# Raw key weights fetched first, three large and 46 small unread products at the start, and a new order for the first 428 operations

## The chip, the core and the metric

The kernel runs on one core of one Trainium2 chip. Five engines work side by side, each on its own list of instructions and in the order of that list: TensorE (PE, matrix products; its weight loads are shown apart as PEld), VectorE (DVE), ScalarE (ACT), GpSimd (POOL) and SyncE (SP, which here issues all transfers). An instruction whose data are not there holds everything behind it on its engine. The metric is the device time of one execution in microseconds; smaller is better.

## What is computed

```python
def phi(x):                                   # features, 64 per position
    a = np.einsum('rd,bhsd->bhsr', S1, x)
    b = np.einsum('rd,bhsd->bhsr', S2, x)
    return np.einsum('bhsi,bhsj->bhsij', a, b).reshape(*x.shape[:-1], r * r)
q_p, k_p = phi(q), phi(k)                     # 4 batches, 4 heads, 1088 positions, 32 wide
kv = np.einsum('bhsf,bhsd->bhfd', k_p, v)
z = np.sum(k_p, axis=2)
x = (q_p @ kv) / (q_p . z + 1e-6)             # heads side by side: 4 x 1088 x 128
h = np.maximum(x @ w_in, 0.0)                 # 128 -> 1024
u, v = h[..., :512], h[..., 512:]
v_n = (v - mean(v)) / np.sqrt(var(v) + 1e-6)  # over the 512
v_s = np.einsum('ts,bsd->btd', w_spatial, v_n) + b_spatial[None, :, None]
out = (u * v_s) @ w_out                       # 512 -> 128
```

`S1`, `S2`, `w_in` and `w_out` arrive as 64-bit floats and are turned into 32-bit ones on the chip; "raw key weights" are `S1` and `S2` in that raw form.

## The kernel before

**Tiling.** Positions are tiles of 128 (nine, the last one half real), three of them to a group g. The outer loop is over the four batches. In batch 0 the chain is: key tiles (`kt0g`) times the weights `sk` (product `kab0g`, L747), a copy (`ka0g`, ACT, L752), features (`kp0g`, DVE, L754), the sum over values (`kv0`, L784), masked into `kd0`; the same for queries (`qab`, `qa`, `qp`), then transposes (`tq`, L833), sums and denominators (`nd`, L847), division (`rec`, `x32`), and x as a high and a low part (`xh0`, `xl0`, L865 and L866). Almost every operand that a product reads is such a pair, made by a cast on ACT and a subtraction on DVE or POOL, and a product is three passes: high-high, high-low, low-high.

The hidden layer gives `pv` (the half that is normalised, one product triple per tile) and `pu` (the other half, one per 128 columns d). `vt` is `pv` after the rectifier (ACT), `st` and `mv` its statistics (DVE, L959, L960), then it is normalised (DVE L995 or ACT L998) and split into `vh` (ACT, L1064) and `vl` (DVE, L1067), one tile of positions at a time for batch 0; the second half of the last tile gets the rest in L1076.

**The spatial product** is the bulk of PE's work: `sp0dc` sums over nine position tiles kt for each column block d (4) and each of three pieces c of the output positions. For batch 0 and c = 0 the four d run side by side in four PSUM banks: first the steps with `vh` and `vl` against the high weights (L1123, L1125), one step of two products per kt and d, the ninth with one product; then those with the low weights (L1132). The transposed spatial weights come in blocks `wt{kt}{c}`, each cast to `wTh` (ACT, L720) and subtracted to `wTl` (DVE or POOL, L724). For c = 1 and 2 and for batches 1 to 3 the d follow each other.

**What sets the order.** Each operation is recorded with its engine, a cost and what it reads and writes. `schedule` then plays the five engines forward and appends, again and again, the operation that can start first; among those that could start nearly together on an engine the due number decides. Due numbers come from two lists of names: `ORDER` for the first 428 operations (up to the first products of batch 0's second piece), free within the slack, and `THEN` for all others, each bound to its engine and its place there. Costs, the transfer rate (`RATE`, `SLOW_AT`, `LATENCY`) and the eight transfers in flight decide what "can start first" means. When PE would wait, the planner puts in filler products that nobody reads (`fill`, L608), as many as it thinks fit. So the program's order on each engine is fixed when it is built; on the chip only waits happen.

**The start.** Two memsets make `z9`; PE multiplies it `N_WARM` times by itself (L596, 128 x 128) and then `N_SMALL` times in 32 x 32 corners (L601); these and the fillers are read by nobody. The raw weights `s_raw` go through seven DVE steps (L643 to L656) to `sk`, which the first projection `kab00` needs with the first key tile. The second half of `w_in` (`wi_raw1`, `wi_x1`) takes the same seven steps on 512 columns; its first half (`wi_raw0`) is loaded into the buffers of the three key tiles once `kab02` has read them, and `w_out` (`wo_raw`, `wo_x`) into them later. The bias row `b32` is split into `bh` and `bl` and sent to the last low weights by two transfers. All 32-bit products that are not split run as two passes on PE, so the trace counts twice as many.

## Time and profile before

| what | before |
|---|---|
| runs, us | 324.51, 324.68, 328.12; median 324.68 |
| the profiled execution, us | 326.01 |
| its span, first to last instruction, us | 324.2 |
| PE busy | 317.2 us, 98% |
| PEld busy | 301.8 us, 93% |
| DVE busy | 226.2 us, 70% |
| ACT busy | 164.8 us, 51% |
| POOL busy | 64.5 us, 20% |
| moved by DMA | 26.82 MB, mean 83 GB/s |

Busy shares are means over the whole span, while the change lies in its first fifth, so stretches of it have to be read one by one. A matmul's end is modelled and matmuls overlap, so a busy PE can still be waiting in part; start-to-start times of the same product, early and late, tell more. An instruction of DVE or ACT overlaps the next by about 0.1 us, so its own time counts from its start to the next one's start ("at pitch").

### The profile page before, as it was taken

What the parts mean: (1) busy time and instruction counts of PE and PEld (TensorE: products, weight loads), DVE (VectorE), ACT (ScalarE), POOL (GpSimd) and SP (SyncE); (2) the same over time, 40 slices, a digit from 0 to 9 for tenths busy, and PEclk for the clock granted to TensorE, in tenths of its full rate; (3) what the DMA queues carried; (4) which work ended last, traced back from release to release, by engine and by line L of the source; (5) the groups of instructions that cost most, each with busy time, mean ns of one, the idle gap of its engine ahead of it and who ended that gap; (6) DMA issues with size and microseconds to landing.
All of it is one profiled execution on the core that took longest, in us unless ns stands there. A gap on an engine that the chain in (4) does not pass through costs nothing.

```text
span 324.2 us, 6830 instructions
## 1 busy us (share of the span) xinstructions
PE 317.2 (98%) x2636; PEld 301.8 (93%) x2636; DVE 226.2 (70%) x512; ACT 164.8 (51%) x391; POOL 64.5 (20%) x81
## 2 busy tenths in 40 slices
PE   8999999999999999999999999999999999999995
PEld 7887999899998999999899999999999999999995
DVE  3999995646799962889884658895325687439382
ACT  3499935525785626566544567462424455416040
POOL 1000005566201035321004702240001321103000
PEclk9999999999999999999999999999999999999999
DMA  7873229462010473011043115001000421000001
GB/s 237 289 243 129 53 58 337 142 209 73 21 52 20 129 230 126 2 40 31 14 120 121 61 51 168 0 2 42 3 0 0 128 64 42 2 1 2 0 1 69
DMA packets 21548, 26.82 MB, mean 83 GB/s; under 512 B 2828, under 2 KB 21260, under 8 KB 21516
## 3 DMA queue, kind: packets, MB, share of 16 engines
q1 hardware_dynamic: 21516, 26.39, 26.1%
q8 instruction: 20, 0.33, 0.4%
q14 instruction: 12, 0.10, 0.1%
HBM read 23.31 MB, written 3.06 MB: 81 GB/s over the span
## 4 chain that ended last, share of the span: by engine, by line
PE 77%; DVE 7%; ACT 6%; DMA 6%; issue 2%; SPq 1%; POOL 0%; POOLq 0%; DVEq 0%; ACTq 0%
PE sp L1123 15%; PE sp L1125 13%; PE sp L1132 13%; PE sd L1357 4%; DMA pl<-in_wT 4%; PE sp L1357 3%; PE sd L573 3%; PE sd L575 3%; PE sd L574 3%; PE pu L573 2%; PE po L574 2%; PE po L573 2%; PE pu L575 2%; PE pu L574 2%; PE po L575 2%; PE sp L1134 2%
## 5 line engine op out<-in xcount | busy, mean ns | idle before, releaser
L1123 PE MATMUL sp<-wTh,vh 128*128 128x332 f32 (+1 forms) x350 | 115.0, 329 | 0.0
L1125 PE MATMUL sp<-wTh,vl 128*128 128x332 f32 (+1 forms) x304 | 99.1, 326 | 0.0
L1123 PEld LDWEIGHTS sp<-wTh,vh 128*128 128x128 f32 x350 | 65.8, 188 | 2.6 <-issue 1.2
L1132 PE MATMUL sp<-wl,vh 128*128 128x332 f32 x192 | 59.9, 312 | 0.0
L1125 PEld LDWEIGHTS sp<-wTh,vl 128*128 128x128 f32 x304 | 57.1, 188 | 0.7
L1132 PE MATMUL sp<-wTl,vh 128*128 128x424 f32 x112 | 37.1, 349 | 0.0
L660 ACT CAST g<-u 128x332 fp32r<-128x332 f32 (+1 forms) x41 | 19.8, 490 | 32.5 <-DVE u L1160 22.3
L1132 PEld LDWEIGHTS sp<-wl,vh 128*128 128x128 f32 x192 | 36.0, 188 | 0.0
L583 DVE TENSOR_TENSOR g<-u,g 128x332 fp32r<-128x332 f32 (+1 forms) x41 | 23.1, 562 | 18.0 <-PE po L574 11.4
L1160 DVE TENSOR_TENSOR u<-sp,u 128x332 f32<-128x332 f32 (+1 forms) x43 | 22.4, 521 | 15.9 <-PE sp L1134 9.5
L933 DVE RECIPROCAL c<-c 128x384 f32<-128x384 f32 (+1 forms) x9 | 21.8, 2419 | 16.3 <-ACT c L931 16.3
L1115 ACT ACTIVATE u<-pu 128x332 f32<-128x332 f32 (+1 forms) x44 | 20.6, 469 | 22.2 <-PE pu L575 17.7
L1036 ACT CAST vh<-vt 128x384 fp32r<-128x384 f32 x36 | 17.3, 511 | 20.7 <-DVE vt L995 11.7
L902 POOL TENSOR_TENSOR pl<-pl,pl 128x384 f32<-128x384 f32 (+1 forms) x18 | 18.1, 1007 | 39.6 <-DMA pl<-qd 39.6
L959 DVE BATCH_NORM_STATS2 st<-vt 128x6 f32<-128x512 f32 x36 | 24.0, 684 | 2.2 <-ACT vt L957 1.9
L586 POOL TENSOR_TENSOR r<-pl,r 128x384 fp32r<-128x384 f32 (+1 forms) x18 | 17.7, 986 | 38.3 <-ACT r L660 36.1
L957 ACT ACTIVATE vt<-sd 128x512 f32<-128x512 f32 x36 | 21.4, 603 | 7.5 <-PE sd L575 6.7
L1038 DVE TENSOR_TENSOR vl<-vt,vh 128x384 fp32r<-128x384 f32 (+1 forms) x36 | 18.1, 512 | 5.3 <-ACT vh L1036 5.2
L1132 PEld LDWEIGHTS sp<-wTl,vh 128*128 128x128 f32 x112 | 21.0, 188 | 0.1
L724 POOL TENSOR_TENSOR wl<-pl,wTh 128x332 fp32r<-128x332 f32 x8 | 7.5, 953 | 49.8 <-ACT wTh L720 49.7
L573 PE MATMUL pu<-xh,wih 128*128 128x332 f32 (+1 forms) x48 | 16.5, 343 | 0.0
L995 DVE TENSOR_SCALAR vt<-vt,mv,sm 128x512 f32<-128x512 f32 x32 | 16.4, 557 | 0.0
(287 smaller groups left out, 668.1 us busy)
## 6 DMA issues: line engine op xcount, KB each, us to landing
pl<-in_wT SPq DMA_DIRECT2D x34, 166.0 KB
v<-in_vA SPq DMA_DIRECT2D x12, 198.0 KB
kt<-in_kT SPq DMA_DIRECT2D x12, 192.0 KB
pl<-qd SPq DMA_DIRECT2D x12, 192.0 KB
pl<-qd SPq DMA_DIRECT2D x24, 96.0 KB
c<-in_qT SPq DMA_DIRECT2D x9, 192.0 KB
wl<-in_wT SPq DMA_DIRECT2D x8, 212.0 KB
out<-u SPq DMA_DIRECT2D x6, 166.0 KB
```

The costliest lines, as they stand in the source:

```text
L573: nc.tensor.matmul(o, ah, bh, start=start, stop=False)
L574: nc.tensor.matmul(o, ah, bl, start=False, stop=False)
L575: nc.tensor.matmul(o, al, bh, start=False, stop=stop)
L583: return lambda: nc.vector.tensor_tensor(out=o(), in0=a(), in1=bb(), op=ALU.subtract)
L933: op("DVE", 135 + 6.3 * n, lambda x32=x32, n=n: nc.vector.reciprocal(out=x32[:, :n], in_=x32[:, :n]), w=[x32])
L957: op("ACT", c_act(512, True), lambda pv=pv, t=t: nc.scalar.activation(vt[:, t], pv.ap, AF.Relu), r=[pv], w=[(vt, t)])
L959: op("DVE", 690, lambda stats=stats, t=t: nc.vector.bn_stats(out=stats.ap, in_=vt[:, t]), r=[(vt, t)], w=[stats])
L1123: nc.tensor.matmul(sp[:, :cw], vh[:, kt], wTh[:, kt, cs], start=(kt == begin), stop=False)
L1125: nc.tensor.matmul(sp[:, :cw], vl[:, kt], wTh[:, kt, cs], start=False, stop=False)
L1132: nc.tensor.matmul(sp[:, :cw], vh[:, kt], w_lo(kt, c), start=False, stop=False)
L1160: op("DVE", c_dve(cw), lambda: nc.vector.tensor_tensor(out=u.ap, in0=sp[:, :cw], in1=u.ap, op=ALU.mult), r=[sp], w=[u], lead=LEAD[1])
L1357: nc.tensor.matmul(x[:, :cw], p, q, start=i == 0 and n == 0, stop=end and i == 3 and n == 2)
```

## The change

Five edits, all in what the planner is given; no operation of the computation is added or taken away.

- `N_WARM` goes from five to three, `N_SMALL` from 36 to 46.
- The planner's model of transfers: a higher rate, one rate for the transfers through DRAM, and a list of pauses in place of one late slow-down.
- The planner's cost of the small products, of the first projection, and the size of `w_in`'s transfers.
- `ORDER`, the 428 names, is another list. `THEN` is the same.

```diff
-N_WARM = 5
-N_SMALL = 36
+N_WARM = 3
+N_SMALL = 46
...
-kt00:1 z9:1 eps:2 z9:2 s_raw:1 eps:1 v93:1 wps:1 v90:1 kt01:1 wps:2 v92:1 v91:1 wps:3 wi_raw1:1 wps:4
+s_raw:1 z9:1 eps:2 z9:2 kt00:1 eps:1 v92:1 wps:1 v91:1 kt01:1 wps:2 v93:1 v90:1 wps:3 b32:1 wps:4
...
-RATE, SLOW_AT, SLOW_BY, LATENCY = 0.265, 4000, 500, 1500
+RATE, BOUNCE, LATENCY = 0.38, 0.13, 1500
+PAUSES = ((3500, 1050), (8000, 900), (13000, 1400), (18000, 1400), (49000, 900), (51800, 800), (57200, 2000))
...
-                dma = max(dma, s + cost + LATENCY) + o.kb / (RATE if o.kb > 0 else -0.12)
+                dma = max(dma, s + cost + LATENCY) + o.kb / (RATE if o.kb > 0 else -BOUNCE)
...
-                if dma > SLOW_AT and not slow:
-                    slow, dma = True, dma + SLOW_BY
+                while pauses and dma > pauses[0][0]:
+                    dma += pauses.pop(0)[1]
...
-    op("PE", 1300, f4=True, fn=small, r=[z9], w=[wps], due=0)
+    op("PE", 1770, f4=True, fn=small, r=[z9], w=[wps], due=0)
...
-        load(raw, lambda: raw[:, :1024].bitcast(U32), w_in[:, sl].bitcast(U32), 640)
+        load(raw, lambda: raw[:, :1024].bitcast(U32), w_in[:, sl].bitcast(U32), 524)
...
-        op("PE", 353, f4=True, fn=lambda: project(ab, xt), r=[xt, (sk, "x")], w=[ab])
+        op("PE", 353 + (300 if ab.name == "kab00" else 0), f4=True, fn=lambda: project(ab, xt), r=[xt, (sk, "x")], w=[ab])
```

Lines of the new kernel stand one further on than before (L747 is L748).

**First place: the start of PE's list**, from the first unread product to the sum over values (`sd`: projections and unread products; `po`: fillers; `pu`: the sum over values). Before:

```order
L596 MATMUL sd_161<-u_87 128x128 x5
L601 MATMUL sd_161<-u_87 32x32 x36
L608 MATMUL po_222<-u_87 128x64
L747 MATMUL sd_224<-sk,kt 64x2x32 x6
L747 MATMUL sd_161<-sk,kt 64x2x32 x6
L608 MATMUL po_222<-u_87 128x64 x8
L747 MATMUL sd_224<-sk,kt 64x2x32 x6
L747 MATMUL sd_161<-sk,c_124 64x2x32 x6
L608 MATMUL po_222<-u_87 128x64
L784 MATMUL pu_273<-v,kp_93 32x33 x24
```

Of the change:

```order
L597 MATMUL sd_161<-u_87 128x128 x3
L602 MATMUL sd_161<-u_87 32x32 x46
L748 MATMUL sd_228<-sk,kt 64x2x32 x6
L748 MATMUL sd_161<-sk,kt 64x2x32 x6
L609 MATMUL po_253<-u_87 128x64 x5
L748 MATMUL sd_228<-sk,kt 64x2x32 x6
L748 MATMUL sd_161<-sk,c_124 64x2x32 x6
L609 MATMUL po_253<-u_87 128x64 x3
L785 MATMUL pu_282<-v,kp_93 32x33 x24
```

The filler ahead of the first projection is gone, five stand ahead of the third instead of eight, and three ahead of the values instead of one.

And **the start of SP's list of transfers** (`pl` from `in_sks`: raw key weights; `b`: bias row; `vt` and `kt` from `in_w_in`: the two halves of the input weights; `c`: query tiles; `wl` and `pl` from `in_wT`: spatial weights). Before:

```order
L580 DMA kt<-in_kT 128x384
L580 DMA pl_145<-in_sks 128x128
L580 DMA kt<-in_kT 128x384
L580 DMA vt_90<-in_w_in 128x1024
L580 DMA kt<-in_kT 128x384
```

Of the change:

```order
L581 DMA pl_145<-in_sks 128x128
L581 DMA kt<-in_kT 128x384 x2
L581 DMA b_132<-in_bsp 72x16
L581 DMA vt_90<-in_w_in 128x1024
L581 DMA kt<-in_kT 128x384
```

Further on in SP's list, before:

```order
L580 DMA u_88<-in_idn 128x128
L580 DMA c_125<-in_qT 128x384
L580 DMA kt<-in_w_in 128x1024
L580 DMA c_126<-in_qT 128x384
L580 DMA wl_103<-in_wT 128x424
```

Of the change:

```order
L581 DMA u_88<-in_idn 128x128
L581 DMA c_125<-in_qT 128x384
L581 DMA wl_111<-in_wT 128x424
L581 DMA c_126<-in_qT 128x384
L581 DMA kt<-in_w_in 128x1024
L581 DMA wl_105<-in_wT 128x424
```

The raw key weights are first, the bias row fourth instead of ninth, and one block of spatial weights and the last query tile stand ahead of the first half of the input weights.

**Second place: DVE around the first low part of x** (`xl`, L866; `wTl`: low spatial weights; `kp`: features; `sm`: denominators; `c`: x before the split; `v`: steps on the input weights). Before:

```order
L851 TENSOR_SCALAR sm_68<-sp_377 128x12
L852 RECIPROCAL sm_68<-sm_68 128x12
L646 TENSOR_SCALAR v<-v 128x512
L854 TENSOR_TENSOR c_125<-sp_377,sm_68 128x384
L648 TENSOR_SCALAR v<-v 128x512
L754 TENSOR_TENSOR kp_95<-ka_86,sd_161 128x768
L866 TENSOR_TENSOR xl_119<-sp_413,xh_117 128x384
L724 TENSOR_TENSOR wTl_102<-wl_103,wTh 128x424
```

Of the change:

```order
L755 TENSOR_TENSOR kp_95<-ka_86,sd_161 128x768
L852 TENSOR_SCALAR sm_68<-sp_393 128x12
L725 TENSOR_TENSOR wTl_110<-wl_111,wTh 128x424
L853 RECIPROCAL sm_68<-sm_68 128x12
L584 TENSOR_TENSOR wil<-vt_91,wih 128x512
L855 TENSOR_TENSOR c_125<-sp_393,sm_68 128x384
L647 TENSOR_SCALAR v<-v 128x512
L725 TENSOR_TENSOR wTl_104<-wl_105,wTh 128x424
L725 TENSOR_TENSOR wTl_116<-pl_146,wTh 64x424
L649 TENSOR_SCALAR v<-v 128x512
L867 TENSOR_TENSOR xl_119<-sp_425,xh_117 128x384
```

Three subtractions for low spatial weights, which stood behind the first `xl`, are ahead of it, and the last feature product has moved ahead of the denominators.

**Third place: DVE up to the last rest of the normalised values** (`vh`, L1076; `vl`: low parts of the values; `vt`: normalisation). Before:

```order
L1067 TENSOR_TENSOR vl<-vt_90,vh 128x4x128
L995 TENSOR_SCALAR vt_91<-vt_91,mv_82,sm_73 128x512 x2
L1067 TENSOR_TENSOR vl<-vt_91,vh 128x4x128 x2
L1076 TENSOR_TENSOR vh<-vt_91,vh 64x4x128
L724 TENSOR_TENSOR wTl_114<-wl_115,wTh 128x424
L724 TENSOR_TENSOR wTl_100<-wl_101,wTh 128x424
L724 TENSOR_TENSOR wTl_108<-wl_109,wTh 128x424
```

Of the change:

```order
L725 TENSOR_TENSOR wTl_100<-wl_101,wTh 128x424
L987 SCALAR_TENSOR_TENSOR sm_74<-mv_82,sm_73 128x3
L725 TENSOR_TENSOR wTl_106<-wl_107,wTh 128x424
L996 TENSOR_SCALAR vt_91<-vt_91,mv_82,sm_73 128x512 x2
L647 TENSOR_SCALAR v<-v 128x512
L1068 TENSOR_TENSOR vl<-vt_91,vh 128x4x128 x2
L649 TENSOR_SCALAR v<-v 128x512
L725 TENSOR_TENSOR wTl_108<-wl_109,wTh 128x424
L650 SCALAR_TENSOR_TENSOR v<-kt,v 128x512
L1077 TENSOR_TENSOR vh<-vt_91,vh 64x4x128
```

Here too subtractions for low spatial weights (`wTl_100`, `wTl_108` and others), which stood behind L1076, are ahead of it; steps on the output weights (`v`) stand between.

## Rows read from the trace of the kernel before

**Rows 1.** The page, part 2: GB/s moved in 40 equal slices of 8.1 us.

```profile
GB/s 237 289 243 129 53 58 337 142 209 73 21 52 20 129 230 126 2 40 31 14 120 121 61 51 168 0 2 42 3 0 0 128 64 42 2 1 2 0 1 69
```

**Rows 2.** Stretches: length; busy us (instructions) of five engines; clock, DMA.

```profile
12.00:32.00 20.00, 19.45 (x143) 15.77 (x143) 19.89 (x53) 18.47 (x44) 0.00 (x0) 1.00 0.67 219
32.00:44.00 12.00, 12.00 (x65) 11.56 (x64) 11.56 (x33) 10.33 (x25) 0.00 (x0) 1.00 0.15 39
...
60.00:70.00 10.00, 9.54 (x192) 8.94 (x192) 5.47 (x7) 4.08 (x11) 6.20 (x6) 1.00 0.41 127
70.00:320.00 250.00, 249.30 (x1845) 240.11 (x1833) 170.65 (x379) 121.65 (x288) 51.80 (x62) 1.00 0.18 53
```

**Rows 3.** Order of time, first 8 us: start, us, engine line operation [wait].

```profile
0.74 0.40 SPq L580 DMA_DIRECT2D kt<-in_kT  x1
...
1.20 0.41 SPq L580 DMA_DIRECT2D pl<-in_sks  x1
...
1.32 2.50 PE L596 MATMUL sd<-u 128*128 128x128 f32 x10 [1.32 <-DVE u L592]
...
3.38 0.20 DVE L645 TENSOR_SCALAR sk<-pl 128x64 uint32<-128x64 uint32 x1 [2.11 <-DMA pl<-in_sks]
...
3.75 1.19 PE L601 MATMUL sd<-u 128*32 128x32 f32 x72
...
4.81 0.23 DVE L656 TENSOR_TENSOR sk<-sk 128x64 f32<-128x64 f32 x1
...
5.49 1.30 PE L747 MATMUL sd<-sk,kt 128*64 128x64 f32 x24
...
6.72 1.82 DVE L754 TENSOR_TENSOR kp<-ka,sd 128x768 f32<-128x768 f32 x2 [1.68 <-ACT ka L752]
```

**Rows 4.** Order of time, PE alone, 1 to 13 us.

```profile
6.73 2.00 PE L608 MATMUL po<-u 128*128 128x64 f32 x16
8.65 0.57 PE L747 MATMUL sd<-sk,kt 128*64 128x64 f32 x12
9.05 0.52 PE L747 MATMUL sd<-sk,c 128*64 128x64 f32 x12
...
9.87 1.53 PE L784 MATMUL pu<-v,kp 128*32 128x33 f32 x144
```

**Rows 5.** Stretches, 9 to 10 us; at the end clock, DMA, GB/s.

```profile
9.00:10.00 1.00, 1.00 (x37) 0.86 (x36) 0.80 (x2) 0.58 (x3) 0.00 (x0) 1.00 0.15 52
```

**Rows 6.** Order of time, DVE alone, first low part of x.

```profile
17.56 0.56 DVE L866 TENSOR_TENSOR xl<-sp,xh 128x384 fp32r<-128x384 f32 x1
```

**Rows 7.** Order of time, DVE alone: first L1067 and L1076.

```profile
30.84 0.66 DVE L1067 TENSOR_TENSOR vl<-vt,vh 128x512 fp32r<-128x512 f32 x1
...
41.91 0.69 DVE L1076 TENSOR_TENSOR vh<-vt,vh 64x512 fp32r<-64x512 f32 x1
```

**Rows 8.** Line L724: shortest/median/longest ns, first and last start.

```profile
L724 DVE TENSOR_TENSOR wTl<-wl,wTh x8: 590/596/601, 18.0 to 46.0; 128x424 fp32r<-128x424 f32 x8
```

**Rows 9.** The page, part 5: statistics, normalisation; busy us, mean ns.

```profile
L959 DVE BATCH_NORM_STATS2 st<-vt 128x6 f32<-128x512 f32 x36 | 24.0, 684 | 2.2 <-ACT vt L957 1.9
...
L995 DVE TENSOR_SCALAR vt<-vt,mv,sm 128x512 f32<-128x512 f32 x32 | 16.4, 557 | 0.0
```

**Rows 10.** Order of time, PE alone: the first spatial product.

```profile
31.23 0.82 PE L887 MATMUL sd<-c,sk 128*64 128x192 f32 x8
31.98 0.46 PE L1123 MATMUL sp<-wTh,vh 128*128 128x424 f32 x1
```

**Rows 11.** Order of time, PE alone: the product behind L1076.

```profile
43.14 0.35 PE L1123 MATMUL po<-wTh,vh 128*128 128x424 f32 x1
```

**Rows 12.** Line L643, first step on output and input weights, ACT.

```profile
L643 ACT ACTIVATE v<-kt x2: 680/713/746, 14.4 to 33.9; 128x512 f32<-128x512 f32 x2
```

**Rows 13.** Chain of waits, 47 to 64 us: start, us, what.

```profile
53.69 5.91 DMA pl<-in_wT
...
61.39 1.28 DVE xl L583
```

More of the change, by code (lines that the diff above doesn't have):

```diff
@@ new lines @@
+wi_x1:3 qa00:1 kp02:1 wt20:1 kv0:1 wi_x1:4 wt80:1 kv0:2 qp00:1 wTl:11 kv0:3 wt00:1 wi_x1:5 qab01:1 wt30:1 kd0:1
+tq00:1 wTh:6 wi_x1:6 wTl:10 tq01:1 qa01:1 qab02:1 wt40:1 qpT00:1 qp01:1 qpT01:1 qa02:1 nd00:1 wi_x1:7 qp02:1 wih:1
+tq10:1 rec0:1 wTl:6 tq11:1 wt01:1 wi_x0:1 tq20:1 rec0:2 wt70:1 wil:1 wTh:3 wt60:1 x320:1 qpT10:1 qpT11:1 wt11:1
+tq21:1 wi_x0:2 wTh:9 xt0:1 wTl:3 wt10:1 nd01:1 wTh:1 wTl:9 wt21:1 xh0:1 wt31:1 wi_x0:3 wTh:5 xl0:1 wt41:1
+wTh:4 rec1:1 wi_x0:4 wt51:1 pv000:1 wTh:10 rec1:2 wi_x0:5 pv001:1 x321:1 qpT20:1 qpT21:1 vt00:1 wt61:1 wi_x0:6 xt1:1
@@ new lines @@
+wTh:8 st000:1 nd02:1 vt00:2 wo_raw:1 xh0:2 wi_x0:7 wTh:7 xl0:2 wih:2 pv002:1 rec2:1 mv00:1 rec2:2 wTh:2 wil:2
+pv010:1 wTh:11 x322:1 vt00:3 pu000:1 st001:1 wTh:15 qt10:1 xt2:1 vt01:1 st002:1 qt11:1 pv011:1 u000:1 qt12:1 mv00:2
+mv00:3 xh0:3 st010:1 pv012:1 sd00:1 wo_x:1 rs00:1 xl0:3 pu010:1 vt01:2 t100:1 wTl:2 vt01:3 pv020:1 t100:2 st011:1
+u010:1 pv021:1 wTh:13 rs00:2 st012:1 vt02:1 pu020:1 nm00:1 mv01:1 vt02:2 vt00:4 pv022:1 u020:1 vt00:5 vh00:1 pab10:1
+st020:1 vh00:2 pu030:1 vl00:1 vt02:3 mv01:3 vl00:2 sp010:1 vt00:6 sp000:1 mv01:2 st021:1 sp020:1 sd01:1 wTh:16 sp030:1
@@ new lines @@
+rs01:1 wTh:14 st022:1 sp010:2 vh00:3 sp030:2 t101:1 mv02:2 t101:2 wTh:12 mv02:3 sp000:2 rs01:2 wTl:13 abT10:1 pab11:1
+nm01:1 qd10:1 vl00:3 vt01:4 pab12:1 sp020:2 mv02:1 qd10:2 vt01:6 sd02:1 vh00:4 sp030:3 rs02:1 wt71:1 vt01:5 sp010:3
+abT11:1 vl00:4 vh00:6 sp020:3 qd11:1 sp000:3 vh00:5 t102:1 vl00:6 qd11:2 sp020:4 sp010:4 t102:2 vl00:5 sp030:4 abT12:1
+sp000:4 qd12:1 rs02:2 wTl:1 wTh:17 sp010:5 qd12:2 nm02:1 wTl:4 sp030:5 vt02:4 sp010:6 vt02:5 sp020:5 vt02:6 vh00:7
+sp030:6 wo_x:2 vh00:8 sp000:5 vl00:7 sp000:6 v91:2 v93:2 sp020:6 vl00:8 v92:2 v90:2 sp030:7 vh00:9 wo_x:3 sp010:7
@@ new lines @@
+u010:2 sp020:16 v11:1 sp020:17 sp000:16 wTl:18 g010:1 sp000:17 v12:1 sp000:18 sp020:18 wTh:19 wt52:1 kab10:1 u000:2 wTh:20
+wTl:21 wt62:1 u020:2 g000:1 g010:2 wTh:21 sp030:15 wt72:1 wTh:22 sp030:16 g000:2 sp001:1 kt20:1 ka10:1 u030:1 sp001:2
+kt21:1 wTl:22 ka11:1 wTh:23 sp030:17 kt22:1 sp001:3 wTl:23 wt82:1 pu001:1 sp001:4 u001:1 wTl:24 fa100:1 sp001:5 wTh:24
+sp001:6 wTl:25 fb100:1 po00:1 wTh:26 fb100:2 sp001:7 wTl:26 g020:1 sp001:8 fa101:1 sp001:9 sp030:18 fb101:1 sp011:1 u001:2
+po00:2 u030:2 gh001:1 sp011:2 gl001:1 g030:1 sp011:3 wTh:27 sp011:4 sp011:5
```

34 lines of the change are left out of this document (7 added, 27 removed).

## The prediction, made before the changed kernel ran

> **What bounds the kernel now.** I read the page first, then busy time by stretch, then the first microseconds in order of time, then the chain of waits. From 70 to 320 us TensorE (PE) is busy for 249.30 of 250 us [rows 2], and the order of that part is fixed by the table that the change leaves alone. So the change can only move the moment at which PE enters that part, and any move there is carried to the end.
>
> Ahead of it stand two stretches. Up to 12 us PE mostly waits for data or makes unread products. From 12 to 32 us three engines are full together: VectorE (DVE) 19.89 of 20 us, ScalarE (ACT) 18.47, PE 19.45 [rows 2]. Which of them has slack? [...] DVE decides between them: at 19.89 of 20 it cannot give back anything unless it starts earlier or does less ahead of what PE waits for. I therefore reckon by DVE's queue.
>
> The execution that was profiled took 326.01 us (span 324.2, 1.8 around it); the median of the runs shown is 324.68. All terms below are differences, which I take from the median.
>
> **The start.** Now the first transfer is a key tile and the second the raw key weights, issued at 1.20; DVE's seven steps on them run from 3.38 to 5.04; PE fills the time with five large and 36 small unread products and one filler pair, and the first projection starts at 5.49; the first feature product on DVE starts at 6.72 [rows 3]. After, the weights are issued first, at 0.74, 0.46 us sooner. Nothing is then ahead of them on the DMA engines, where 192 KB of key tile were. Gain for DVE's first step: at least the 0.46 of the issue, at most another 0.83, which is 192 KB at the 237 GB/s of the first slice [rows 1]. I take 0.7, nearer the low end, since the trace does not show how much of a transfer's time depends on what is ahead. DVE's seven steps then end at 4.35.
>
> PE must be free by then. Each product is two passes. Ten large passes take 2.43 us up to the first small one, 0.21 to 0.24 each; four fewer put that at about 2.85. 72 small passes take 1.19 us, 92 take 1.5: over at 4.35. The filler pair between 4.94 and 5.49 is gone from there. So the projection starts at about 4.45 instead of 5.49: **1.0 us** sooner, bounded by 0.8 (weights only 0.46 sooner) and 1.1 (PE's small products end it). The two warm-up edits (0.9 us less, 0.3 us more of PE) thus end together with DVE's steps, which are their cover; if the weights come sooner still, the small products are what is paid, bit by bit.
>
> The bias row's split moves ahead too: one cast on ACT before the first key copy, one subtraction of 0.17 us on DVE before the first feature product. Both fall into idle time there (DVE is idle from 5.04 to 6.72 [rows 3]); if the bias row, now fourth in the queue, reached ACT later than about 5.0, every bit of that would be paid, because the key copies stand behind it on ACT. With 256 KB landed DVE started at 3.38; the bias row has 192 KB more ahead, 0.83 us, so some 4.2: nothing.
>
> **The gap at 9 us.** Eight filler pairs (16 passes) stand ahead of the third projection, from 6.73 to 8.65 [rows 4]. Five stand there after, from 5.7, so it runs at about 7. In the queue, the second half of the input weights needs the key buffers that the third projection reads; so the queue stands behind it and DMA falls to 0.15 of its time from 9 to 10 us [rows 5]. After, a block of spatial weights and a query tile go ahead of it, and the third projection is 1.6 us sooner. Some 0.85 us of DMA time is won for every later weight block. It ends no wait of DVE, which is full, so I count it as nothing for the end; it is the cover for the next term, where those blocks are needed earlier.
>
> **DVE's queue.** DVE has no idle time to speak of from the first feature product to 32 us, so each later step stands at its old time, minus 1.0, plus the work that the new order puts ahead of it. I summed the durations ahead of each mark, each instruction by its own start-to-start in the trace:
> - First low part of x (L866), 17.56 [rows 6]. Three subtractions on spatial weights come ahead of it, 0.50 us each at pitch (0.60 long [rows 8], overlapping by 0.1), less the bias: +1.35. So 17.9, 0.35 later than before, though the start is 1.0 earlier.
> - First low part of the normalised values (L1067), 30.84 [rows 7]. One weight subtraction and one normalisation (0.45 at pitch) come in, one statistics step (0.60) and three small ones go behind [rows 8, 9], the bias (0.12) has moved: -0.04. So 29.8.
> - The last rest of the values (L1076), 41.91 [rows 7]. Three weight subtractions net and one normalisation [rows 8, 9], some 2.15 us: +2.15. So 43.05, 1.15 later.
> ACT has one step on the output weights, 0.7 us [rows 12], more ahead of its first cast of the normalised values (smaller differences cancel); its 1.53 us of idle time from 12 to 32 [rows 2] may or may not take that up.
>
> **What PE makes of it.** Its first spatial product is at 31.98 [rows 10]. After, it needs the 29.8 plus 0.66 for that DVE step [rows 7]: 30.5, or up to 31.2 when ACT's 0.7 is paid in full; I take 30.8. Two transposed projections (0.75 us [rows 10]), now done before, follow only after seven spatial steps, so PE is really 0.43 ahead. Before the product that needs L1076 it now has 31 spatial steps and those projections. In the kernel before, that product stands at 43.14 [rows 11] after 29 steps, 0.385 us each. So 30.8 + 0.75 + 31 x 0.385 = 43.5. L1076 ends at 43.05 + 0.69 = 43.7, so PE waits 0.2. With two steps more the kernel before would be at 43.9. PE is 0.2 ahead when this stretch ends. Bounds: 0.7 ahead (no wait), 0.6 behind (ACT paid and DVE 0.8 worse).
>
> **The wait at 62 us.** A late weight block (in the chain 5.91 us of DMA from 53.69) holds ACT's queue, and DVE's split, on which PE's last output product of that round waits, runs from 61.39 to 62.67 [rows 13]; PE has 9.54 busy of 10 us there [rows 2]. After, that block is issued ahead of two key tiles instead of behind them. It wins the 0.46 or nothing; I take 0.3.
>
> Sum: 324.68 - 0.2 - 0.3 = **324.2 us**.
>
> **The rivals.**
> 1. My case, the start's gain mostly eaten by DVE's extra work ahead: 323.5 to 324.7. Chance 0.52.
> 2. Slower: DVE's queue decides at the last rest of the values. It pays as soon as the start wins less than about 0.7 or the weight rows that DVE and ACT now take early land after their turn, since an engine that waits in order holds everything behind it (for instance ACT's weight cast ahead of the query copies). If L1076 ends at 44.7 instead of 43.7, PE is 0.8 behind instead of 0.2 ahead, and the late wait stays: 324.68 + 0.8 = 325.5. For it: +2.15 us and a full DVE. Against: low products that need only finished data stand just behind. Chance 0.30.
> 3. All of it arrives: DVE finds idle time in the new order, PE never waits, and the wait at 62 us goes: 324.68 - 1.0 - 0.46 = 323.2. [...] Against: +2.15 at L1076. Chance 0.12.
> 4. PE's clock rises later. [...] Chance 0.06.
>
> **How the numbers follow.** Predicted 324.2, my case. The range 323.0 to 325.6 takes in cases 1 and 3 and most of case 2; what is left out is the top of 2, and part of 4: under 2 in 10. My case alone is 323.5 to 324.7. 2% is 6.5 us, about what a measurement of this kernel can tell from no change; the first projection cannot start before the weights have landed, and from 5.49 to 12 us there are only 6.5 us in all, so no case reaches it: within 2% 0.97, faster 0.01, slower 0.02 (a transfer that lands several microseconds late).
>
> **What would show it.** Right: DVE's first step on the weights at 2.5 to 2.9, the first projection at 4.3 to 4.7, the first feature product by 5.9; the third projection before 7.2; DMA above half its time from 9 to 10; L1067 first at 29.5 to 30.5 and L1076 at 42.7 to 44. Wrong: a first feature product after 6.2 (bias or clock), PE idle over 0.5 us between 36 and 44, or the start's full 1.0 us still there at 44 us. If PE's busy time falls between 70 and 320 us, the assumption that the rest is carried unchanged is wrong.

## The result: slower by about 1%, and the profile after

The changed kernel took **328.74 us** (median; 327.51 to 330.55) against 324.88 for the kernel before, measured beside it, a ratio of 1.010 with an interval of 1.0055 to 1.0148. Taken once more it was 1.012 (1.0084 to 1.0158). That is still within 2%, but outside the predicted 323.0 to 325.6, and on the other side of zero. Executions more than 1.5% above the fastest of their own kernel (two of `a_warm`, one of `a_warm_kt02`) are left out of the medians and ratios below.

The profiled execution took 328.73 us (span 326.9, 2.7 more than before). First its first microseconds, in order of time (start, length, engine, line, operation, count, wait):

```profile
0.74 0.39 SPq L581 DMA_DIRECT2D pl<-in_sks  x1
...
2.52 0.20 DVE L646 TENSOR_SCALAR sk<-pl 128x64 uint32<-128x64 uint32 x1 [1.26 <-DMA pl<-in_sks]
...
2.90 1.50 PE L602 MATMUL sd<-u 128*32 128x32 f32 x92
...
4.48 0.20 ACT L661 CAST bh<-b 72x16 fp32r<-72x16 f32 x1 [2.25 <-DMA b<-in_bsp]
...
5.26 1.82 DVE L755 TENSOR_TENSOR kp<-ka,sd 128x768 f32<-128x768 f32 x2 [0.37 <-ACT ka L753]
```

The start came as forecast, and slightly more: against [rows 3] the first step on the weights is 0.86 us sooner and the first feature product 1.46 sooner. Then PE alone, 4 to 19 us:

```profile
4.33 0.96 PE L748 MATMUL sd<-sk,kt 128*64 128x64 f32 x24
5.22 1.33 PE L609 MATMUL po<-u 128*128 128x64 f32 x10
8.79 0.91 PE L748 MATMUL sd<-sk,kt 128*64 128x64 f32 x12 [2.25 <-DMA kt<-in_kT]
10.01 0.91 PE L748 MATMUL sd<-sk,c 128*64 128x64 f32 x12 [0.31 <-DMA c<-in_qT]
10.85 1.54 PE L609 MATMUL po<-u 128*128 128x64 f32 x6
12.33 2.21 PE L785 MATMUL pu<-v,kp 128*32 128x33 f32 x144
...
16.63 1.64 PE L848 MATMUL sp<-u,c 128*128 128x66 f32 x12
18.10 1.15 PE L834 MATMUL po<-u,kp 128*128 128x128 f32 x9
```

From 6.54 to 8.79 us PE waits for the third key tile. The third projection is at 8.79 instead of 8.65 [rows 4] or the forecast 7, and the values' products, 9.87 before, are at 12.33: 2.46 later, though the first projection was 1.16 sooner. The trace's clock records read full from 4.45 us, half from 7.87 and full again from 14.69. The stretches show it too (length, busy us of PE, PEld, DVE, ACT, POOL, then clock, DMA share, GB/s):

```profile
5.49:12.00 6.51, 3.95 (x40) 3.57 (x39) 3.99 (x6) 1.22 (x4) 0.00 (x0) 0.68 0.94 292
12.00:32.00 20.00, 19.07 (x271) 16.28 (x271) 18.21 (x45) 16.26 (x38) 0.00 (x0) 0.93 0.69 227
32.00:44.00 12.00, 12.00 (x68) 10.50 (x68) 11.51 (x38) 10.58 (x24) 0.00 (x0) 1.00 0.15 39
60.00:70.00 10.00, 10.00 (x66) 9.95 (x65) 4.97 (x9) 4.67 (x11) 5.06 (x7) 1.00 0.51 166
70.00:320.00 250.00, 249.21 (x1956) 239.97 (x1956) 171.20 (x378) 122.73 (x290) 53.06 (x63) 1.00 0.19 55
```

Against [rows 2], DVE has lost 1.68 us of busy time from 12 to 32: the engine by which the prediction reckoned was not full any more. The three marks on DVE, the first spatial product and the one that needs L1077, and the place of the wait at 62 us, in order of time:

```profile
21.73 0.54 DVE L867 TENSOR_TENSOR xl<-sp,xh 128x384 fp32r<-128x384 f32 x1
```

```profile
33.90 0.69 DVE L1068 TENSOR_TENSOR vl<-vt,vh 128x512 fp32r<-128x512 f32 x1 [0.22 <-ACT vh L1065]
```

```profile
46.67 0.69 DVE L1077 TENSOR_TENSOR vh<-vt,vh 64x512 fp32r<-64x512 f32 x1
```

```profile
34.58 0.35 PE L1124 MATMUL po<-wTh,vh 128*128 128x424 f32 x1
...
47.41 0.46 PE L1124 MATMUL po<-wTh,vh 128*128 128x424 f32 x1
```

```profile
65.48 0.35 PE L574 MATMUL po<-xl,woh 128*128 128x424 f32 x1
65.67 0.35 PE L575 MATMUL po<-xl,woh 128*128 128x424 f32 x1
```

The marks were 17.56, 30.84 and 41.91 [rows 6, 7]: later by 4.2, 3.1 and 4.8. The first spatial product is at 34.58 instead of 31.98 [rows 10], the one behind L1077 at 47.41 instead of 43.14 [rows 11]. At 65.48 the last output product of that round runs on without the 0.46 us of waiting that PE had there before, at 62.25 (it follows on `xl`, [rows 13]). At the start of the steady part PE is 2.8 us behind the kernel before, and 2.7 at the end: all of it is lost ahead of 66 us.

### The profile page after: what moved, and what is told of

It reads as the page before. It is cut to its first block, busy times and chain, and to the rows that moved or that the text cites. A ratio compares the mean times of both kernels' runs of the same rounds, so it can differ in the third digit from the quotient of the medians.

```text
span 326.9 us, 6871 instructions
## 1 busy us (share of the span) xinstructions
PE 317.9 (97%) x2652; PEld 302.4 (93%) x2652; DVE 227.3 (70%) x513; ACT 165.1 (51%) x390; POOL 64.2 (20%) x81
## 4 chain that ended last, share of the span: by engine, by line
PE 79%; DMA 7%; DVE 6%; ACT 3%; SPq 2%; issue 1%; DVEq 0%; ACTq 0%
PE sp L1124 16%; PE sp L1133 14%; PE sp L1126 13%; PE sd L1358 4%; PE sp L1358 3%; PE sd L574 3%; PE sd L576 3%; PE sd L575 3%; DMA pl<-in_wT 3%; PE pu L574 2%; PE po L575 2%; PE po L574 2%; PE po L576 2%; PE sp L1135 2%; SPq L581 2%; PE pu L575 2%
## 5 line engine op out<-in xcount | busy, mean ns | idle before, releaser
L1133 PE MATMUL sp<-wl,vh 128*128 128x332 f32 x192 | 59.9, 312 | 0.0
L584 DVE TENSOR_TENSOR g<-u,g 128x332 fp32r<-128x332 f32 (+1 forms) x41 | 22.4, 546 | 16.7 <-PE po L575 12.7
L1116 ACT ACTIVATE u<-pu 128x332 f32<-128x332 f32 (+1 forms) x44 | 20.6, 468 | 21.7 <-PE pu L576 16.5
```

The costliest lines, as they stand in the source:

```text
L584: return lambda: nc.vector.tensor_tensor(out=o(), in0=a(), in1=bb(), op=ALU.subtract)
L1116: op("ACT", c_act(cw, True), lambda: nc.scalar.activation(u.ap, pu[:, :cw], AF.Relu), r=[pu], w=[u], lead=LEAD[0])
L1133: nc.tensor.matmul(sp[:, :cw], vh[:, kt], w_lo(kt, c), start=False, stop=False)
```

## The experiments

Each kernel is the one before (names in `b_`) or the changed one (`a_`), with the planned order edited by hand: `ahead(x, y)` puts operation x in front of y, a *pair* is one unread filler product (L608; two passes in the trace). "Fell" counts executions with a mean granted clock under 0.997; it was none of the 94 executions of the kernel before that were taken beside these kernels. (An expectation below says 11 of 18 for the changed kernel and one variant; it is 13 of 18, and 10 of 13 for the changed kernel alone.) *New start* means raw key weights first, three large unread products and no pair ahead of the first projection; the *head* is what follows up to the values' products: pairs, the bias row and a few transfers.

| kernel | median, us | ratio to before | fell |
|---|---|---|---|
| changed, once more | 329.11 | 1.0121 (1.0084 to 1.0158) | 10 of 13 in all |
| `a_fill` nine more pairs | 332.08 | 1.0207 (1.0180 to 1.0233) | 6 of 6 |
| `a_kt02` third key tile fourth | 329.04 | 1.0105 (1.0084 to 1.0125) | 4 of 6 |
| `a_warm` 5 large, 18 small | 329.33 | 1.0137 (1.0079 to 1.0194) | 3 of 5 |
| `a_warm_kt02` both | 329.55 | 1.0121 (1.0089 to 1.0153) | 3 of 5 |
| `a_tail` new start, old head, new order | 328.96 | 1.0111 (1.0070 to 1.0152) | 2 of 6 |
| `a_best` the same, lighter | 328.78 | 1.0105 (1.0080 to 1.0130) | 4 of 6 |
| `b_start` new start, old order | 325.65 | 1.0013 (0.9986 to 1.0039) | 1 of 11 |
| `b_head` new start and head, old order | 327.11 | 1.0070 (1.0049 to 1.0091) | 5 of 6 |
| `b_best` new start, lighter | 325.29 | 1.0001 (0.9982 to 1.0020) | 7 of 12 |
| `b_start_lean` lighter still | 325.58 | 1.0016 (0.9999 to 1.0034) | 7 of 12 |
| `b_warm` 3 large, 46 small | 325.36 | 1.0009 (0.9981 to 1.0037) | 0 of 11 |
| `b_nofill` no pairs at 7 us | 327.64 | 1.0057 (1.0033 to 1.0081) | 7 of 12 |
| `b_tiny` eight small for eight pairs | 324.98 | 0.9995 (0.9978 to 1.0013) | 0 of 12 |
| `b_code` 60 small instead of 36 | 330.03 | 1.0141 (1.0095 to 1.0187) | 6 of 6 |
| `b_four` 4 large, 30 small | 326.77 | 1.0046 (1.0011 to 1.0081) | 6 of 12 |

### First round: the idle time at 7 us

> The changed kernel once more, unaltered. In its profiled execution TensorE had nothing to do from 6.54 to 8.79 us, its granted clock read half from 7.87 to 14.69 us, and from the first spatial product on everything lay some 2.8 us behind the kernel before. Theory C (the fallen clock is the cause): whenever the third key projection comes late enough to leave TensorE idle for some 2 us, half clock follows, and the time is 327 to 331 us, 2.5 to 6 above the kernel before; an execution in which the projection comes by 7.5 us keeps full clock and ends near 324. Theory Q (DVE's longer queue is the cause, as in the second rival of the prediction): the time is above the kernel before by 0.8 us or more in each execution, whatever the clock does.

```diff
+one = order[fillers("kab02:1")[0]]
+order[at("kab02:1"):at("kab02:1")] = [one] * 9
```

> The changed kernel with nine more unread products ahead of the third key projection (14 instead of 5), so that TensorE is busy while it waits for the third key tile; nothing else differs. Theory C: the granted clock stays at full from 4.5 us on; the third projection still comes at about 8.8 us, if its tile lands as late as before, and the values' products and the first transposed projection come at 10 and 12.3 us (2 to 3 us sooner than in the changed kernel); the first spatial product at 31 to 32 instead of 34.6, and the time at 323.5 to 325.5 us, that is 2.5 to 5 below the changed kernel. Theory Q: the time moves by less than 0.7 us, since DVE's queue ahead of the spatial products is as long as before. Theory L (the late landing alone, through the engines that wait for the third tile): no change either, the tile is as late as before.

```diff
+ahead("kt02:1", "b32:1")
```

> The changed kernel with one transfer moved: the third key tile is issued fourth, ahead of the bias row and of the first half MB of input weights, instead of sixth. Theory L (and C, by way of the idle time): the tile lands by 6 us, the third projection runs at 6.6 to 7.2 us, there is no idle time of 2 us, the clock stays at full, and the time is 323.5 to 325 us. If the time is that of the changed kernel (327 or more) although the projection comes at 7 us, the cause lies behind it, in DVE's queue (theory Q) or in the input weights that now land later (192 KB more ahead of them, about 0.8 us). What it could not tell apart alone, C from L, the run with nine more unread products does.

```diff
+for n in reversed(fillers("kab02:1")):
+    del order[n]
```

> The kernel before without the eight pairs of unread products that stand ahead of its third key projection (from 6.73 to 8.65 us); nothing that is read is left out. TensorE then idles from about 6.8 to 8.65 us. Theory C: the granted clock falls to half at some 8 us and stays there for several microseconds, the first transposed projection (12.02 before) comes 1 to 3 us later, and the time is 326.5 to 328, 2 to 3 us above the kernel before, with its old order and its old start. Theories Q and L: no difference, 324.5 to 325, since those products give nothing to anyone.

The repeat's profile has no idle time at 7 us and took 328.60 all the same. PE in order of time:

```profile
5.86 2.40 PE L609 MATMUL po<-u 128*128 128x64 f32 x10
8.18 0.91 PE L748 MATMUL sd<-sk,kt 128*64 128x64 f32 x12
...
10.45 1.54 PE L609 MATMUL po<-u 128*128 128x64 f32 x6
11.92 2.20 PE L785 MATMUL pu<-v,kp 128*32 128x33 f32 x144
```

Ten filler passes take 2.40 us here and 1.33 in the first profile: the clock record of this execution begins only at 13.98 us. No execution came near 324, as theory C had it for full clock: the three of the changed kernel that did not fall have a median of 328.6, the ten that did 328.9, and all 13 are 327.5 or more, as theory Q asks. So the mean clock alone does not sort them; what follows separates the causes. The clock is at half up to 14 us in both profiles (from 7.87 on in the first), once because it fell, once because it rose late (six filler passes take 1.54 us in both, at the recorded half of the first and ahead of the record of the repeat), and the fillers that the planner put ahead of the third projection and the values then are on the path themselves. Moving the key tile (`a_kt02`) did not change the median either: its clock record begins at 13.85. Its profile is 0.94 us ahead of the changed kernel's at 71 us, and no longer ahead at the end: 0.3 of it goes at 124 us, 0.3 in a longer stall at 173 us, 0.2 at 269 us.

The two others gave what no theory expected. `a_fill` is 3 us slower still: PE stands still for 2.07 us in the middle of the third query projection, at 14.46, and the profile names no releaser but "issue". `b_nofill` is 1.2 us ahead of the kernel before at 70 us, and loses 2.3 at 116 us inside the values' products of a later batch:

```profile
PE sd L784 <- issue: 2.3, 1, 2.3
```

### Second round: the products at the start

```diff
+order[at("wps:1"):at("wps:1")] = [order[at("wps:1")]] * 2
-N_SMALL = 46
+N_SMALL = 18
```

> The changed kernel with other unread products at its start: five large and 18 small instead of three large and 46 small, about as long (ten large passes 2.4 us, 36 small 0.6); nothing else differs. In the repeat of the changed kernel the clock record begins only at 13.98 us and unread pairs took 0.43 us up to there and 0.2 behind, in the kernel before the record begins at 6.37; no idle time of 2 us stood there. Theory W (the lighter unread products at the start let the granted clock rise late): the record begins by 7 us, the third projection comes at 8.2, the values' products by 10.5, the first spatial product at 31.5 to 32.5 instead of 34.1 to 34.6, and the time is 325.5 to 327 us, 2 to 3 below the changed kernel. Theory O (the new order of DVE, ACT and the queue is the cause): the same time as the changed kernel, 328.5 to 330.

```diff
+(as a_warm)
+ahead("kt02:1", "b32:1")
```

> The changed kernel with five large and 18 small unread products, and with the third key tile issued fourth, ahead of the bias row and the first half MB of input weights. Theory W: the clock rises by 7 us and does not fall again, because TensorE is nowhere idle for 2 us; time 324.5 to 326 us, 3 to 4.5 below the changed kernel, and up to 1 below the run with the other unread products alone. Theory O: 328.5 to 330, as the run with the key tile moved alone (329.04).

```diff
+del order[at("wps:1")], order[at("wps:2")]
-N_SMALL = 36
+N_SMALL = 46
```

> The kernel before with the changed kernel's unread products at the start (three large and 46 small instead of five large and 36 small); order, queue and all else as before. The products end about 0.6 us sooner, and the time that is left up to the first projection (5.2 to 5.5) is idle. Theory W: the granted clock rises later than 6.4 us in most executions, unread pairs ahead of the third projection take 0.43 instead of 0.24 us, the first transposed projection comes 1 to 3 us later than 12.02, and the time is 326.5 to 328.5 us. Theory O: 324.5 to 325.7, no difference.

```diff
+(as b_warm)
+ahead("s_raw:1", "kt00:1")
+del order[fillers("kab00:1")[0]]
```

> The kernel before with the start of the changed one: raw key weights issued first, three large and 46 small unread products, no unread pair ahead of the first projection; the order of all later work as before. First projection at 4.3 to 4.5 us. Theory O: the gain of the start with the old order, 323.5 to 324.7 us. Theory W: the clock rises late (after 7 us in most executions), and the time is 325.5 to 328 us.

In the profile of `a_warm`, of an execution of 334.31 us, the clock did rise at 6.26 and the values' products began at 9.47, sooner than in the kernel before. Then this (PE, order of time):

```profile
9.47 1.23 PE L785 MATMUL pu<-v,kp 128*32 128x33 f32 x111
14.50 0.67 PE L785 MATMUL pu<-v,kp 128*32 128x33 f32 x33 [3.80 <-issue]
```

After 111 of 144 passes PE stops for 3.80 us although all data are there, and the clock falls at 13.09. Whether the executions nearer its median stop there too is not shown. The lighter products did not make `b_warm` slower, nor `b_start`: theory W as a rule for all executions falls.

What "issue" is can be read from the trace. Part 3 of the changed kernel's page has this line (packets, MB, share):

```profile
q8 instruction: 21, 0.34, 0.4%
```

Queue q8 fetches 16 KB at a time, 21 times for 2652 PE passes: one piece per 126 passes with their weight loads. I counted the passes ahead of each stall of 0.5 us or more that is put down to "issue", up to 200 us, in all profiles of this study: 221 (`a_warm`, `a_warm_kt02`), 347 or 348 (`a_fill`, `b_warm`, `b_head`, `a_tail`, `after_third`, `b_code`), 856 (`a_fill`), 1236 or 1237 (`b_nofill`, `a_warm`, `a_warm_kt02`, `b_four`) and 1744 or 1745 (the changed kernel and four others, in the values' products at 170 to 175 us), and no other count. (The kernel before has a shorter one, 0.40 us, at 1745.) The steps between them, 126, 509, 380 and 508, are 1, 4, 3 and 4 pieces. In `a_warm` the packet of q8 starts at 12.23 and takes 0.88; PE goes on 1.39 later.

So I read such a stall as PE reaching the end of one piece before the next has arrived: in `a_warm` PE stood still from 10.70 to 14.50, and the packet came in between, from 12.23 to 13.11. How many pieces PE can hold at once is not shown.

### Third round: head against order, and the instructions

```diff
+ahead("b32:1", "v01:1"); ahead("bh:1", "kv0:1"); ahead("bl:1", "kv0:2")
+(pairs: 8 ahead of kab02, 1 ahead of kv0)
```

> The changed kernel's order from the third projection on, with the head of the kernel before ahead of it: the bias row's transfer, cast and rest back at their old places, eight unread pairs ahead of the third projection and one ahead of the values' products (5 and 3 in the changed kernel); the new first transfer and the new unread products stay. Its counterpart with the old order behind the same start took 325.65 us, the changed kernel 328.7 to 329.1. Theory T (the order behind the head costs most): 327 to 328.5 us. Theory H (the head costs most, through TensorE's idle time, the fallen clock and the bias row ahead): 325 to 326.3. In the two profiles with half clock up to 14 us the changed kernel ends 1.2 us behind its counterpart at 67 us, so I expect 326.5 to 327 and thus both in part.

```diff
+(as b_start)
+ahead("b32:1", "wi_raw1:1"); ahead("mask_sb:1", "qt00:1"); ahead("bh:1", "ka00:1")
+ahead("bl:1", "kp00:1"); ahead("wt50:1", "kab02:1"); ahead("qt02:1", "wi_raw0:1")
+(pairs: 5 ahead of kab02, 3 ahead of kv0)
```

> The counterpart: the kernel before with the changed kernel's whole head (raw key weights first, bias row fourth with its cast and rest ahead of the first key copies, a spatial block and a query tile ahead of the second half of the input weights, three large and 46 small unread products, five unread pairs ahead of the third projection and three ahead of the values' products) and the old order behind it. Theory H: 327 to 328.5 us, with a clock that falls back in most executions, as in the changed kernel (mean granted clock below 0.997 in 11 of 18 executions there, in none of the kernel before). Theory T: 325 to 326, as with the start alone (325.65).

```diff
-matmul(home[:, :64], z9, z9[:, :64])         # the eight pairs ahead of kab02
+matmul(home[:32, :32], z9[:, :32], z9[:, :32])
```

> The kernel before with the eight unread pairs ahead of its third projection replaced by eight small unread products (32x32 instead of 128x64), so that TensorE has as many instructions as before but 1.7 us less work there. Without those pairs at all the profile was 1.2 us ahead of the kernel before at 70 us and then lost 2.3 us at 116 us, in the middle of a block of values' products, with nothing but the engine's own issue ahead of it. Theory F (TensorE's instructions come in 16 KB pieces on a queue of their own, and it stands still where it reaches the end of a piece before the next has come; what counts is how many instructions lie ahead of the dense values' products): with the old count there is no stall at 116 us, the 1.2 us last to the end, and the time is 323.5 to 324.5, 1 us below the kernel before. Theory G (idle time ahead of the third projection costs it later, through the clock): 326.5 to 328, as without the pairs (327.64).

```diff
+(as b_start; one small product ahead of kab02 in place of the eight pairs)
```

> The kernel before with the changed start (raw key weights first, three large and 46 small unread products, no pair ahead of the first projection) and one small unread product in place of the eight pairs ahead of the third projection, so that the count of TensorE's instructions is that of the kernel before at each product behind it. The third projection then comes when its tile lands, at about 7 us instead of 8.65. Theory F: the start's gain arrives in part, since the third piece of instructions was late by 1.07 us at 15 us where the start was sooner; no stall behind that; 323 to 324.5 us. Theory G: idle time of 1.4 us ahead of the projection lets the clock rise late or fall in most executions: 326 to 328.

Both halves cost, and they do not add up: the new head with the old order is 1.0070, the new order behind the old head 1.0111, both together 1.010 to 1.012. Each half's profile has a stall behind 347 or 348 passes in it, 0.82 us in `b_head` and 1.21 in `a_tail`, so neither ratio is the price of head or order alone. `b_tiny` shows that the eight pairs were not needed for the clock (none of 12 fell), and that with the old count of passes the stall at 116 us is gone; of the 1.2 us of `b_nofill` only 0.4 are left at 70 us, and the median is that of the kernel before. `b_start_lean` was profiled in an execution of 323.88 us with full clock from 6.16 on: 1.8 us ahead of the kernel before at 71 us. Its median is 325.58. The clock fell in 7 of 12, but these have a median of 325.59 and the other five 325.42, so what takes the gain in most executions is not shown. In `b_nofill` and `b_best` a fall does part them: 328.02 against 326.23, and 325.88 against 324.54.

### Fourth round: one head, two orders; one program, two clocks

```diff
+(as b_start; 4 pairs ahead of kab02; N_SMALL = 43)
```

> The kernel before with the changed start (raw key weights first, three large unread products) and four unread pairs ahead of the third projection instead of eight, 43 small products instead of 46, so that as many of TensorE's instructions stand ahead of each later product as in the kernel before. The four pairs fill the time in which the engine was idle with one small product there (6.12 to 7.00 us). Theory C (half clock in the first 15 us is what takes the start's gain): the clock falls back in fewer executions than there (7 of 12 below 0.997), and the time is 323.9 to 324.8, 0.5 to 1.2 below the kernel before. Theory T (only the order matters, the head is worth nothing either way): 325 to 325.7.

```diff
+(as a_tail; 4 pairs ahead of kab02; N_SMALL = 43)
```

> The same head with the changed kernel's order behind it: new start, bias row at its old places, four unread pairs ahead of the third projection, one ahead of the values' products, 43 small products. What it lies above its counterpart with the old order (the other kernel of this call) is the price of the order alone, with as little trouble from the clock and from late instructions as I can arrange. Theory T: 1 to 2.5 us above it, 325.5 to 327. Theory C (the order is harmless, half clock is all): within 0.6 of it. My prediction's sum had 0.8 for the order (the start's gain of 1.0 less the 0.2 that was left).

> One more profile of the kernel before with the changed start. Its first profile was an execution of 327.00 us in which full clock is recorded only from 14.31 us; eight of its eleven executions took 324.7 to 325.9. Theory C: an execution of that kind shows full clock from 5 to 7 us on, and up to 70 us it is 1.5 to 2.5 us ahead of the first profile, all of it won between 5 and 15 us. Otherwise (the clock does not matter) it differs elsewhere, at a transfer or behind 15 us.

> One more profile of the changed kernel, unaltered. Theory C: with full clock from 5 to 7 us on and no fall, 326 to 327.5 us, and the first spatial product near 32; with a late rise or a fall as in the first two profiles, 328 to 330. Theory F (late instructions): where the clock is full early, TensorE stands still for 0.5 us or more at the first denominators (about 15 us), where the fourth piece of its instructions begins.

The two profiles of `b_start` price the clock inside one program. PE, order of time, first profile (clock record from 14.31), then second (from 4.78):

```profile
5.80 3.68 PE L608 MATMUL po<-u 128*128 128x64 f32 x16
...
11.51 2.21 PE L784 MATMUL pu<-v,kp 128*32 128x33 f32 x144
```

```profile
5.38 2.00 PE L608 MATMUL po<-u 128*128 128x64 f32 x16
...
9.51 1.78 PE L784 MATMUL pu<-v,kp 128*32 128x33 f32 x144
```

At the values' products the second is 2.0 us ahead, at 71 us still 2.0 (70.41 against 72.38 for the same spatial product). So half clock up to 14 us costs 2 us that nothing up to there gives back. At the end 1.6 are left (spans 325.1 and 323.6): the second has a stall of 0.60 us at 170 us, behind 1745 passes, which the first does not have.

The third profile of the changed kernel shows what an early clock does not cure (PE, order of time):

```profile
15.17 1.17 PE L848 MATMUL sp<-u,c 128*128 128x66 f32 x9
18.01 0.44 PE L848 MATMUL sp<-u,c 128*128 128x66 f32 x3 [1.67 <-issue]
```

Its clock rose at 6.46 and fell only from 9.87 to 13.29; PE was at the first denominators 1.0 to 1.5 us sooner than in the other two profiles, and stopped behind 347 passes, as theory F asked. In the three profiles the next pass starts at 17.82, 17.34 and 18.01 us, and q8's packet for it ends at 16.20, 15.84 and 16.66, 1.35 to 1.6 sooner. So the piece arrives just when a slow PE gets there, and the fast PE of the third profile waits for it. In the kernel before, the same count is reached at 16.64, behind the third query projection and the second transposes, with its packet over at 13.48: 3.2 us between, where 1.3 to 1.6 are enough. Ahead of the first denominators the changed kernel has 24 more passes (338 against 314): 12 by the unread products and pairs, and 12 because the third query projection has moved ahead of the denominators.

`a_best` against `b_best` prices the order with one head: 328.78 against 325.29, 3.5 us in the medians, more than either theory gave. Their profiles differ by 1.0 us at 71 us and 2.5 in the span. From the last third of the values' products to 71 us, the profiles without a stall of 0.5 us need 60.3 to 60.6 us in the new order (changed kernel, its repeat, `a_kt02`, `a_best`) and 59.3 to 59.9 in the old one with the new start (`b_start` twice, `b_start_lean`, `b_best`). So about 0.8 us is the order itself; `b_start` and the first two profiles of the changed kernel, all at half clock to about 14 us, give the same (59.5 against 60.3). Between 71 us and the end `a_best` loses another 1.5 to `b_best`: 0.6 in a stall behind 1744 passes, 0.4 at 268 us, where PE waits for ACT (`u`, L1116), the rest in slips at 234 and 286 us. How the difference of the medians is shared between clock and stalls in the executions without a profile stays open.

### Last round: instructions alone

```diff
-N_SMALL = 36
+N_SMALL = 60
+del order[fillers("kab00:1")[0]]
```

> The kernel before with 24 more small unread products at its start (60 instead of 36) and without the one pair ahead of the first projection, so that 46 more of TensorE's passes stand ahead of all later work; nothing else differs. In the profiles so far each stall put down to the engine's own issue lies at one of four counts of passes, 221 to 222, 346 to 348, 1236 to 1237 or 1744 to 1745, whatever the kernel; in the kernel before pass 347 is the third transposed value product at 16.6 us, with the packet of that piece at 12.54. Here pass 347 falls on the second transposed projection at about 12.5 us, 2.3 us after pass 221. Theory F: TensorE stands still there for 2 to 4 us, up to 14.6 to 16.6, and the time is 327.5 to 330 us. Theory C or T: only the first projection is later, by 0.3 us: 325.2 to 326.

```diff
+ahead("s_raw:1", "kt00:1"); del order[at("wps:1")], order[fillers("kab00:1")[0]]
-N_SMALL = 36
+N_SMALL = 30
+(pairs: 6 ahead of kab02)
```

> A try at a version that keeps the start's gain: the kernel before with the raw key weights first, four large and 30 small unread products, no pair ahead of the first projection and six ahead of the third; 20 passes fewer than in the kernel before stand ahead of the values' products, so that pass 221 falls into their second third and pass 347 on the second denominators' product, at 15 to 16 us. Theory F: the start's gain passes that point, 323.8 to 324.8 us in executions with an early clock. Theory C alone: the heavier unread products than in the changed start let the clock rise early in most executions, so a median of 324.3; if the median is 325 or more, this start does not hold the clock either.

`b_code` changes the count of unread passes and nothing that is read. PE, order of time:

```profile
11.92 0.87 PE L833 MATMUL po<-u,kp 128*128 128x128 f32 x6 [0.62 <-DVE kp L754]
12.73 0.33 PE L747 MATMUL sd<-sk,c 128*64 128x64 f32 x2
14.56 0.51 PE L747 MATMUL sd<-sk,c 128*64 128x64 f32 x10 [1.50 <-issue]
```

Up to 12 us it is level with the kernel before (11.92 against 12.02 for the first transposes). Behind 348 passes it stops for 1.5 us (forecast 2 to 4), the clock then falls from 16.38 to 19.79, and it is 2.6 us behind at 71 us. The median is 1.014 (1.0095 to 1.0187); the profile is of the fastest of its six executions, 327.80 us, and the clock fell in all six. Late instructions are a cause of their own. `b_four`, with 20 passes fewer, moved the same trouble to 1237 passes, inside the values' products at 117 us, and was no better:

```profile
PE sd L784 <- issue: 2.9, 1, 2.9
```

No version beat the kernel before beyond its interval.

## Why the prediction was wrong, step by step

- **The start: right.** Forecast 1.0 us for the first projection, measured 1.16 (4.33), a little over the stated bound of 1.1. The bias row, fourth in the queue, reached ACT at 4.48; in the repeat the first key copy came at 5.66 behind it, the case that the prediction named as paid.
- **The gap at 9 us: the first step that failed.** "The third projection runs at about 7" took for granted that PE's fillers held it back. Its tile can: the projection waits for it up to 8.79 in the first profile, 8.10 in `b_start_again`, 7.91 in `b_best` and 7.00 in `b_start_lean`; in `after_third`, at 7.41, it does not wait. The sum had no term for a late projection. The fillers were costed at full clock (five pairs, 1.3 us), while at half clock they take 2.4.
- **The two warm-up edits "end together with DVE's steps, which are their cover": the second failed step.** I priced 20 more small passes by their duration and found cover for it. What they also do was not in the sum: they shift every later product by 16 passes (12, with the pairs that go) against the 16 KB pieces of PE's instructions. In `b_code`, which changes only unread products, a shift by 46 costs 1.5 us at once and 2.6 by 71 us. The page of before had the row (q8 in part 3); I did not use it.
- **Rival 4, the clock: the right effect, too small a chance, a cause that is not shown.** Half clock costs 2.0 us by 71 us inside one program (the two profiles of `b_start`; none of it is hidden up to there), and full clock comes late or falls in all three profiles. That the lighter start is the cause is not shown: `b_warm`, with the same three large products, has full clock from 5.23, and the first profile from 4.45. The fall behind idle time was not in the rival. I gave it 0.06; the clock fell in none of 94 executions of the kernel before and in 10 of 13 here.
- **DVE's queue: differences nearly right, base wrong.** From L867 to L1068 I forecast 11.9 us and it was 12.2 (13.3 before); from there to L1077 I forecast 13.25 and it was 12.8 (11.1 before). The work named for that stretch, three subtractions at 0.50 and a normalisation at 0.45, makes 1.95 and not the 2.15 of the sum; measured is 1.7. But "each later step stands at its old time, minus 1.0" holds only while DVE is full, and it was not: 18.21 of 20 us. All three marks came 3.6 to 4.1 us later than forecast.
- **What PE makes of it: right for the order alone.** From the first spatial product to the one behind L1077 I forecast 12.9 us (30.8 to 43.7), with a wait of 0.2; it is 12.83 (34.58 to 47.41), and that product starts just behind L1077's end (47.36). The sum took 0.8 us of the start's 1.0 for the order; the profiles give about 0.8. The medians of `a_best` and `b_best` give more, and that is explained only in part.
- **Rival 2: the right sign by luck.** It had the kernel slower by 0.8 because L1077 would hold PE for about a microsecond more. L1077 held it no longer than in my case; the time went ahead of it.
- **The wait at 62 us: gone, but not by the order.** PE's 0.46 us of waiting vanished, forecast 0.3; it vanished in `b_start` too, which has the old order.
- **The steady part: right for this kernel.** Busy 249.21 against 249.30; 2.8 us behind at its start, 2.7 at its end. That any move there is carried to the end does not hold in general: `a_kt02` lost 0.9 us on the way, `a_best` 1.5 against its counterpart.

So the sum for the profiled execution reads, at 71 us: start -1.16; half clock, fillers at half clock and the late tile +4.05, which makes +2.89 at the last third of the values' products (13.66 against 10.77); wait -0.74 (from the last output product to the next spatial one 0.56 instead of 1.30); order +0.66, which is what is left: +2.81, carried to the end. In the third profile PE is only 1.4 behind at the values' products, and the late instructions take 1.67 more.

## What to carry to other kernels

A start that is won is kept only if everything that PE needs comes sooner as well: data, clock, and its own instructions. Here the first projection came 1.16 us sooner; then PE waited 2.25 us for the third key tile, half clock cost 2.0 us in `b_start`, and late instructions 1.67 in `after_third`. Count PE's passes ahead of dense groups of small products: an unread product that is moved, added or dropped shifts where the next piece of instructions is needed, and the stall ("issue", with all data there) can show a hundred microseconds later (`b_nofill`, with an edit at 7 us, lost 2.3 us at 116). A planner that costs fillers at full clock puts them on the path whenever the clock is at half (ten passes took 2.40 us in the repeat, 1.33 in the first profile); and one profile of a kernel shows one state of the clock, so a second profile of the same program prices it (2.0 us between the two of `b_start`).

## What the runs showed of the chip that I had not expected

- At the start a piece of instructions was fetched only after PE had entered the piece ahead of it: from the end of 221 passes to q8's packet for the piece that begins at 347 it took 2.05 us in the kernel before (10.49 to 12.54) and 4.1 in `after_third` (11.64 to 15.73). The packet took 0.9 us, and where PE had stopped it went on 1.3 to 1.5 us behind it. DMA moved some 330 GB/s of data at that time (12 to 16 us, in the first profiles of both kernels). It need not be PE's start in one piece that asks for the next: in the changed kernel the fourth packet began at 38.75, 0.94 us before PE's 475th pass (39.69), the first of its piece, while DMA moved 39 GB/s (32 to 44 us).
- The granted clock fell to half at 7.87 us, inside PE's idle time from 6.54 to 8.79, and was at half until 14.69 though PE worked again from 8.79. A fall follows stalls behind 348 and 1237 passes too (`b_code` at 16.38, `b_nofill` at 118.61), and there the loss is longer than the stall: 2.6 us for 1.5, and 3.2 for 2.3. Not every stall brings one: there is none behind the 1.07 us of `b_warm` at 16 us.
- The mean granted clock of a run does not show a late rise: the record begins with it. `b_start` reads 1.0 in the profile in which PE was at half clock up to 14.31 us; only the lengths of equal products show that (16 filler passes in 3.68 or in 2.00 us).
